# A routed expert kernel: VectorE's order of choosing an expert, reading counts and scaling

## The chip, the cores and the metric

One core of a Trainium2 chip. The number that counts is the device time of one execution in microseconds; of several runs the median is taken. The engines are TensorE (PE in rows, its weight loads PEld), VectorE (DVE), ScalarE (ACT), GpSimd (POOL) and SyncE (SP, which only issues DMAs). Each runs its own instructions in order and waits for others by semaphores.

## What is computed

Attention with keys and values averaged over groups of 8, and behind it a mixture of 8 experts with one expert for each token:

```python
k_p = k.reshape(B, H, Sp, 8, D).mean(axis=3)      # B, H, S, D = 8, 8, 576, 64
v_p = v.reshape(B, H, Sp, 8, D).mean(axis=3)
attn = softmax(scale * q @ k_p^T);  x = attn @ v_p  # as rows: 4608 x 512
logits = x @ w_gate;  expert_idx = argmax(logits)
gate_w = softmax(logits)[expert_idx]
out[mask] = gate_w * (relu(x[mask] @ w1[e]) @ w2[e])   # for each expert e, mask = its tokens
```

## The kernel before, in words

The first stage (`attention`, to about 190 us of the profile) goes through 36 tiles of 128 tokens, nine for each pair of batch elements. Its order is written out by hand (the tile framework is told not to reorder), so the source order is the order on each engine. In the loop from line 542, tile t does this: TensorE transposes the weights P of tile t (`p_transpose`, L283), makes the scores of tile t+2 (L263, into the PSUM tile pS), transposes q of tile t+3 (L253, into pq), does at most one piece of key or value preparation through the PSUM tile pm (`kv_transpose` L180, `v_expand` L207), and multiplies the weights with the values and the folded gate matrix (`weigh`, L299, into pU, of which there is one). VectorE takes the maximum of the scores (L267, tile mx), subtracts it (L270, sd, after which pS is free), then in `scale` takes the reciprocal of the row sums (L311, r), scales the gate logits (L313, lh) and the rows (L315, xe, after which pU is free). ScalarE copies out of PSUM and does the exponentials (L276 from sd).

Tiles come in batches of three for the choice of expert (`route`, after a batch's last tile). VectorE sums the logits, takes the maximum, subtracts it and marks the largest (L374 rg, L375 rm, L376 rd, L378 rk); two more operations, rn (L379) and ro (L346), make the one-hot choice. In the next tile, right behind `weigh`, TensorE counts the tokens of each expert with matmuls of ro (L356, L359, into pm); VectorE adds the running counts (L361 rp, L362 carry), which frees pm, and GpSimd goes on from rp (L387) to the rows' places and the scatter to DRAM (L406). `steps` is a list of small closures; `weave()` runs the next one, and it stands between the larger VectorE operations. `halves` holds pieces of the averaging of keys and values (L172), which VectorE runs behind the subtraction and behind the scaling of rows; GpSimd does other such pieces, right behind its part of the counting. The last three batches are marked `late`, and are ordered in another way that the change leaves alone.

Before the change the first four operations of the choice run at once, and rn and ro are put into `steps`, where the first `weave()` of the next tile runs them, behind that tile's maximum. The counts of the batch are read in the loop of line 601, behind all of `scale`.

The second stage (`experts`) goes through units of up to 512 tokens of one expert, 13 of them in this run. At a unit's start VectorE inverts the gate sums (L1203) and goes on with the hidden layer (L988, each of them behind ScalarE's L967); SyncE loads the rows and gates of later units (`xload`, `gates`, L1238). For the first unit some of this is done by the first stage.

Of the kernel before, what the change touches and what calls it, by code (L numbers as in the profile page):

```python
# [78 lines left out]
def attention(ctx, outer, tc, q, k, v, wg, w1v, w2v, xs, W, cst, carry, tab, banks):  # L79
# [222 lines left out]
    def scale(t):  # L302

        u4 = (pS if t == NG * NT - 2 else pU)[:, :, 0 : 4 * VW].rearrange("p a (h x) -> p a h x", h=4)
        bt, (t0, _) = [(i, b) for i, b in enumerate(batches) if b[0] <= t][-1]
        i = t - t0
        if i == 0:
            xe[bt] = (p3.tile([P, NB, XR], F32, tag="xe", name=f"xe{bt}"), p2.tile([P, NB, NE, H], F32, tag="lh", name=f"lh{bt}"))
        x, lh = xe[bt]
        r = p2.tile([P, 2, 4], F32, tag="r", name=f"r{t}")  # L310
        nc.vector.reciprocal(out=r, in_=u4[:, :, :, D + NE])  # L311
        weave()
        nc.vector.tensor_tensor(out=lh[:, i].rearrange("p e (a h) -> p a h e", a=2), in0=u4[:, :, :, D : D + NE], in1=r.unsqueeze(3).to_broadcast([P, 2, 4, NE]), op=ALU.mult)  # L313
        weave()
        nc.vector.tensor_tensor(out=x[:, i, 0:DM].rearrange("p (a h d) -> p a h d", a=2, h=4), in0=u4[:, :, :, 0:D],  # L315
                                in1=r.unsqueeze(3).to_broadcast([P, 2, 4, D]), op=ALU.mult)
        weave(1, True)


    steps, halves, ready = [], [], []  # L320
    powers, counts = [], []

    def weave(n=1, half=False):
        if half and halves:
            halves.pop(0)()
        for _ in range(min(n, len(steps))):
            steps.pop(0)()

    def route(bt):
        t0, nb = batches[bt]  # L330
        x, lh = (a[:, 0:nb] for a in xe.pop(bt))
        nm = lambda s: f"{s}{bt}"
        bc = lambda a: a.unsqueeze(2).to_broadcast([P, nb, NE])
        t8 = lambda s, dt=F32: p2.tile([P, NB, NE], dt, tag=s, name=nm(s))[:, 0:nb]
        t1 = lambda s: p2.tile([P, NB], F32, tag=s, name=nm(s))[:, 0:nb]
        late = t0 + nb + 3 >= NG * NT
        lg, d, key, oh, pos = t8("rg"), t8("rd"), t8("rk"), t8("ro", BF16), t8("rp")
        m, km, pf = t1("rm"), t1("rn"), t1("rf")
        ex = exs[bt % 2][:, 0:nb]
        ix = p3.tile([P, NB], I32, tag="ix", name=nm("ix"))  # L340

        V = nc.vector
        G = V if late else nc.gpsimd

        def chosen():
            V.tensor_tensor(out=oh, in0=key, in1=bc(km), op=ALU.is_equal)  # L346
            if late:
                power()

        def power():  # L350
            nc.scalar.activation(out=ex[:, :, 0:NE], in_=d, func=AF.Exp)

        def count():
            bank = pm

            nc.tensor.matmul(bank[:, 0 : nb * NE], lhsT=lstrict, rhs=oh.rearrange("p t e -> p (t e)"), start=True, stop=False, skip_group_check=True)  # L356
            for i in range(nb):
                n = nb - i
                nc.tensor.matmul(bank[:, (i + 1) * NE : (nb + 1) * NE], lhsT=ones, rhs=oh[:, i : i + 1, :].to_broadcast([P, n, NE]),  # L359
                                 start=False, stop=i == nb - 1, skip_group_check=True)  # L360
            V.tensor_tensor(out=pos, in0=bank[:, 0 : nb * NE].rearrange("p (t e) -> p t e", t=nb), in1=carry.unsqueeze(1).to_broadcast([P, nb, NE]), op=ALU.add)  # L361
            V.tensor_tensor(out=carry, in0=carry, in1=bank[:, nb * NE : (nb + 1) * NE], op=ALU.add)  # L362
            if bt == AHEAD:
                V.tensor_scalar(out=tab[:, K_AH : K_AH + 1], in0=carry[:, 0:1], scalar1=512.0, scalar2=None, op0=ALU.is_ge)

        def put():
            for i in range(nb):
                nc.gpsimd.tensor_copy(out=ix[:, i : i + 1], in_=pf[:, i : i + 1])  # L368
                scatter(ix[:, i : i + 1], x[:, i, :])
            if bt == AHEAD:  # L370
                ready.append(bt)

        pick = [
            lambda: V.tensor_reduce(out=lg, in_=lh, axis=AX.X, op=ALU.add),  # L374
            lambda: V.tensor_reduce(out=m, in_=lg, axis=AX.X, op=ALU.max),  # L375
            lambda: V.tensor_tensor(out=d, in0=lg, in1=bc(m), op=ALU.subtract),  # L376

            lambda: V.scalar_tensor_tensor(out=key, in0=d, scalar=0.0, in1=cst["order"].unsqueeze(1).to_broadcast([P, nb, NE]), op0=ALU.is_ge, op1=ALU.mult),  # L378
            lambda: V.tensor_reduce(out=km, in_=key, axis=AX.X, op=ALU.max),  # L379
            chosen,  # L380
        ]
        gate = [
            lambda: V.tensor_reduce(out=x[:, :, DM], in_=ex, axis=AX.X, op=ALU.add),
            lambda: G.tensor_copy(out=x[:, :, DM + 1].bitcast(I32), in_=cst["tok"][:, t0 : t0 + nb]),
        ]
        row = [
            lambda: G.tensor_tensor(out=pos, in0=pos, in1=oh, op=ALU.mult),  # L387
            lambda: V.tensor_reduce(out=pf, in_=pos, axis=AX.X, op=ALU.add),
            put,
        ]  # L390
        if late:

            steps.extend([*pick, count, row[0], *gate, *row[1:]])
        else:
            run(pick[:4])
            steps.append(lambda: run(pick[4:]))
            powers.append(power)

            def counted():
                run([count, row[0], gate[1]])  # L400
                steps.extend([gate[0], row[1], put])

            counts.append(counted)

    def scatter(at, rows):
        apart(nc.gpsimd.indirect_dma_start(out=xs, out_offset=bass.IndirectOffsetOnAxis(ap=at, axis=0), in_=rows, in_offset=None))  # L406
# [64 lines left out]
    def run(fs):  # L471
        for f in fs:
            f()
# [68 lines left out]
    for t in range(total):  # L542
# [55 lines left out]
        if held:  # L598
            steps.clear()
        scale(t)  # L600
        for f in counts[:]:
            counts.remove(f)
            f()
            if t in pools:
                run(kv_pool(*pools.pop(t), nc.gpsimd))
        if t == total - 3:
# [104 lines left out]
def experts(ctx, tc, xs, w1v, w2v, out, tab, W, ident, empty, scr, u0, banks):  # L711
# [15 lines left out]
    with tc.tile_critical():  # L727
# [10 lines left out]
        def entry(eng, a, u, lo, hi):  # L738
            r = regs.get((eng, a, u))
            return eng.value_load(tab[u : u + 1, a : a + 1], min_val=lo, max_val=hi) if r is None else r  # L740
# [414 lines left out]
        def dve_unit(u):  # L1155
# [45 lines left out]

            dve.wait_ge(st[u % 2], 64 * (u // 2 + 1))
            dve.reciprocal(out=GT[:, u, :, 0], in_=GT[:, u, :, 0])  # L1203
            n = entry(dve, K_U, u, 1, 8)
            if u > 0:
                hidden_lo(u)
# [18 lines left out]
        def xload(u):  # L1225


            if u == 2:
                sp.wait_ge(se, 16 * (NE - 2))
            if u >= 2:  # L1230
                sp.wait_ge(Q["P_xt"], 4 * (u - 1))

            rows_of = []

            def gates():

                for s in range(4):
                    sp.dma_start(out=GT[:, u, s, :], in_=xs[ds(rows_of[s], P), DM:]).then_inc(st[u % 2], 16)  # L1238

            def block(s, apart, rows=True):  # L1240
                r = rows_of[s]
                to, sem = XE[u % 2][:, s, :], sx[u % 2][s]
                if rows and apart:
                    for j in range(4):
                        o = slice(32 * j, 32 * j + 32)
                        sp.dma_start(out=to[o].rearrange("p (g d) -> p g d", g=4),
                                     in_=xs[ds(r, P), j * P : (j + 1) * P].rearrange("(g t) d -> t g d", g=4)).then_inc(sem, 16)
                elif rows:
                    sp.dma_start(out=to, in_=xs[ds(r, P), 0:DM]).then_inc(sem, 16)
                    sp.sem_inc(sem, 48)  # L1250
                else:
                    sp.sem_inc(sem, 64)

            rows_of.extend(entry(sp, K_ROW + s, u, 0, NE * CAP - P) for s in range(4))
            n = entry(sp, K_U, u, 1, 8)

            def blocks(apart):
                for s in range(2):
                    block(s, apart)
                with sp.If(n > 4):  # L1260
                    block(2, apart)
                    with sp.If(n > 6):
                        block(3, apart)
                    with sp.Else():
                        block(3, apart, False)
                with sp.Else():
                    for s in range(2, 4):
                        block(s, apart, False)

            if u < 2:  # L1270
                blocks(False)
                return gates()
            with sp.If(entry(sp, K_U, u - 1, 1, 8) > 2):
                blocks(True)
            with sp.Else():
                blocks(False)
            gates()
# [247 lines left out]
```

## Time and profile before

| | us |
|---|---|
| median of 3 runs | 635.15 |
| lowest and highest | 633.09, 635.31 |
| the profiled execution's own time | 631.38 |
| its span | 629.6 |
| TensorE busy in the span | 602.3 |

The span is what the profiler sees from the first to the last instruction; the execution's time is 1.8 us longer. A row of the timeline gives start, duration, engine, line, operation, what it writes and reads; in square brackets stands how long the engine stood idle before it, and who ended that. A matmul's duration includes the emptying of the array, and consecutive ones overlap, so the distance of starts says more than the durations.

### The profile page before, as it was taken

The page shows a single profiled execution, that of the slowest core. Times are in us where ns is not written, and L with a number is a line of the kernel's source. Part 1 is how long each engine was busy: PE and PEld are TensorE (multiplying, and loading weights), DVE is VectorE, ACT ScalarE, POOL GpSimd, SP SyncE. Part 2 cuts the span into 40 slices and gives each one's busy share as a digit, 9 for nine tenths or more (in the row PEclk, how much of TensorE's full clock was granted, in tenths as well). Part 3 has the DMA queues.
Part 4 walks back from the last instruction along what each step waited for, and adds up shares of the span by engine and source line. Part 5 has one row for each costly group of instructions (what it writes and reads, how often), then busy time and mean ns, then how long its engine had stood idle before and what let it go on. Part 6 is the DMA issues. An engine that isn't in the chain of part 4 may idle for free.

```text
span 629.6 us, 13468 instructions
## 1 busy us (share of the span) xinstructions
PE 602.3 (96%) x4412; PEld 513.0 (81%) x4412; DVE 354.4 (56%) x731; ACT 240.2 (38%) x453; POOL 240.7 (38%) x289
## 2 busy tenths in 40 slices
PE   6989999999997999999999999999998999999995
PEld 6778978888876888889898889888897888888994
DVE  7698887889762124467777433854156664133220
ACT  2577666886512014065354311523034641011110
POOL 7457656744421121468445311251107660101101
PEclk9999999999999999999999999999999899999999
DMA  9999996992324930619667551075105453100001
GB/s 326 363 267 258 300 311 209 254 265 70 125 111 135 300 107 2 216 41 297 221 173 267 153 170 36 3 210 167 40 33 164 132 147 71 55 0 36 36 4 53
DMA packets 93937, 96.47 MB, mean 153 GB/s; under 512 B 43102, under 2 KB 74846, under 8 KB 93792
## 3 DMA queue, kind: packets, MB, share of 16 engines
q1 hardware_dynamic: 85808, 74.27, 41.0%
q0 software_dynamic: 7440, 20.50, 8.8%
q8 instruction: 60, 0.98, 0.6%
q14 instruction: 85, 0.70, 0.4%
q10 hardware_dynamic: 544, 0.02, 0.0%
HBM read 72.68 MB, written 26.00 MB: 157 GB/s over the span
## 4 chain that ended last, share of the span: by engine, by line
PE 76%; DVE 6%; issue 5%; DMA 3%; POOL 3%; ACT 3%; SPq 2%; DVEq 0%; ACTq 0%; POOLq 0%
PE pU L881 33%; PE pP L859 20%; PE pq L859 10%; PE pU L299 4%; DMA XE<-in_v_dram 2%; PE pP L283 2%; PE pP L462 2%; POOL dispatched L406 2%; PE pS L263 2%; PE pq L253 1%; SPq L228 1%; ACT W L1057 1%; PE pm L207 1%; DVE mx L267 1%; PE pq L462 1%
## 5 line engine op out<-in xcount | busy, mean ns | idle before, releaser
L881 PE MATMUL pU<-W,H 128*128 128x512 f32 x912 | 216.2, 397 | 0.0
L881 PEld LDWEIGHTS pU<-W,H 128*128 128x128 f32 x912 | 171.3, 188 | 41.0
L859 PE MATMUL pP<-X,W 128*128 128x512 f32 (+3 forms) x748 | 144.0, 347 | 3.7 <-DVEq L1398 1.5
L859 PEld LDWEIGHTS pP<-X,W 128*128 128x128 f32 x748 | 123.6, 189 | 20.4 <-DVEq L1398 2.0
L1349 POOL DMA_INDIRECT out_dram<-Y,GT x51 | 53.0, 1039 | 193.3 <-DVE Y L1170 167.4
L1065 POOL TENSOR_TENSOR W<-ST,W 128x1024 fp32r<-128x1024 f32 x30 | 77.4, 2591 | 89.9 <-ACT W L1057 89.4
L967 ACT ACTIVATE H<-pP 128x512 fp32r<-128x512 f32 (+1 forms) x67 | 35.9, 536 | 196.7 <-PE pP L859 158.1
L1170 DVE TENSOR_SCALAR Y<-pU,GT 128x512 f32<-128x512 f32 x36 | 26.9, 749 | 110.5 <-PE pU L881 109.0
L988 DVE SCALAR_TENSOR_TENSOR H<-pP,H 128x512 fp32r<-128x512 f32 (+2 forms) x73 | 42.1, 579 | 71.5 <-ACT H L967 69.0
L859 PE MATMUL pq<-X,W 128*128 128x512 f32 (+3 forms) x364 | 73.7, 351 | 1.1 <-DVE H L988 0.6
L859 PEld LDWEIGHTS pq<-X,W 128*128 128x128 f32 x364 | 60.8, 191 | 10.1 <-DVE H L988 1.1
L1057 ACT CAST W<-ST 128x1024 fp32r<-128x1024 f32 x56 | 57.1, 1054 | 2.9 <-DMA ST<-in_moe_w_dram 2.9
L299 PE MATMUL pU<-V,pt 110*128 110x146 f32 (+3 forms) x468 | 56.7, 283 | 1.4 <-ACT pt L284 0.8
L299 PEld LDWEIGHTS pU<-V,pt 110*128 110x128 f32 (+3 forms) x468 | 51.4, 179 | 3.1 <-ACT pt L284 1.8
L1065 DVE TENSOR_TENSOR W<-ST,W 128x1024 fp32r<-128x1024 f32 x26 | 46.8, 1801 | 3.5 <-ACT W L1057 2.5
L967 ACT ACTIVATE H<-pq 128x512 fp32r<-128x512 f32 (+1 forms) x33 | 17.8, 541 | 79.5 <-PE pq L859 55.1
L406 POOL DMA_INDIRECT dispatched<-xe,ix x36 | 38.0, 1054 | 15.6 <-POOL ix L368 7.0
L988 DVE SCALAR_TENSOR_TENSOR H<-pq,H 128x512 fp32r<-128x512 f32 (+2 forms) x35 | 20.8, 595 | 28.2 <-ACT H L967 20.3
L284 ACT COPY pt<-pP 110x384 f32<-110x384 f32 x72 | 30.8, 479 | 6.1 <-PE pP L283 4.9
L276 ACT ACTIVATE P<-sd 128x576 f32<-128x576 f32 x36 | 24.8, 689 | 19.3 <-DVE sd L270 16.2
L172 POOL TENSOR_TENSOR raw<-raw 128x768 f32<-128x768 f32 (+1 forms) x18 | 27.0, 1498 | 12.1 <-DMA raw<-in_v_dram 11.4
L267 DVE TENSOR_REDUCE mx<-pS 128x8 f32<-128x576 f32 x36 | 27.1, 752 | 6.8 <-PE pS L263 4.4
(186 smaller groups left out, 621.8 us busy)
## 6 DMA issues: line engine op xcount, KB each, us to landing
ST<-in_moe_w_dram SPq DMA_DIRECT2D x56, 512.0 KB, 4.6
raw<-in_k_dram SPq DMA_DIRECT2D x12, 768.0 KB
raw<-in_v_dram SPq DMA_DIRECT2D x11, 768.0 KB
XE<-dispatched SPq DMA_DIRECT2D x104, 64.0 KB, 2.0
qa<-in_q_dram SPq DMA_DIRECT2D x24, 256.0 KB
w<-in_moe_w_dram SPq DMA_DIRECT2D x8, 512.0 KB
XE<-dispatched SPq DMA_DIRECT2D x15, 256.0 KB, 3.8
qa<-in_q_dram SPq DMA_DIRECT2D x2, 1024.0 KB
```

Source lines behind the costliest of these rows:

```text
L172: return lambda: eng.tensor_tensor(out=out, in0=raw[:, :, 0:n], in1=raw[:, :, n : 2 * n], op=ALU.add)
L267: nc.vector.tensor_reduce(out=mx, in_=s4, axis=AX.X, op=ALU.max)
L284: take(out=pt[t][a][0:R], in_=pPs[a][0:R, 0 : 3 * P])
L299: nc.tensor.matmul(pu[p0 : p0 + n, a, h * VW : (h + m) * VW], lhsT=pt[t][a][0:r, c % 3 * P + p0 : c % 3 * P + p0 + n], rhs=Vs[g % 2][0:r, ...
L406: apart(nc.gpsimd.indirect_dma_start(out=xs, out_offset=bass.IndirectOffsetOnAxis(ap=at, axis=0), in_=rows, in_offset=None))
L859: r = pe.matmul(out=pH[g % 3][:, :m], lhsT=w1s(w, f, k), rhs=x, start=i == 0, stop=i == len(passes) - 1)
L881: r = pe.matmul(out=pY[:, s % 2, :], lhsT=h, rhs=w[:, k * 512 : (k + 1) * 512], start=start and i == 0, stop=stop and i == len(ps) - 1, sk ...
L967: act.activation(out=HH[:, f, o], in_=src[:, o], func=AF.Relu).then_inc(Q["A_h"], 1)
L988: return dve.scalar_tensor_tensor(out=dst[:, f, to], in0=src[:, at], scalar=0.0, in1=f32(HH[:, f, at]), op0=ALU.max, op1=ALU.subtract)
L1057: act.copy(out=(W1H if i < 4 else W2H)[:, o], in_=ST[:, i, :]).then_inc(Q["A_s1" if i < 4 else "A_s2"], 1)
L1065: eng.tensor_tensor(out=(W1L if i < 4 else W2L)[:, o], in0=ST[:, i, :], in1=f32((W1H if i < 4 else W2H)[:, o]), op=ALU.subtract).then_inc( ...
L1349: pool.indirect_dma_start(out=out, out_offset=bass.IndirectOffsetOnAxis(ap=GT[:, u, s, 1:2].bitcast(I32), axis=0), in_=Y[:, s, :], in_offs ...
```

## The change

The whole choice is made at once behind the batch's last tile. The counts are read behind the reciprocal of the next tile, ahead of scaling logits and rows; what follows the counts (the `tails`) goes into `steps` where it went before. In the second stage a drain is put behind the inversion of the gate sums, and SyncE waits for a unit's first hidden piece before it loads the gates of the unit after the next.

```diff
@@ scale(t)
         nc.vector.reciprocal(out=r, in_=u4[:, :, :, D + NE])
+        for f in counts:
+            f()
         weave()
         nc.vector.tensor_tensor(out=lh[:, i]..., op=ALU.mult)
@@ route(bt), batches that are not late
-            run(pick[:4])
-            steps.append(lambda: run(pick[4:]))
+            run(pick)
             powers.append(power)
-
-            def counted():
-                run([count, row[0], gate[1]])
-                steps.extend([gate[0], row[1], put])
-
-            counts.append(counted)
+            counts.append(lambda: run([count, row[0], gate[1]]))
+            tails.append([gate[0], row[1], put])
@@ the loop over tiles
         scale(t)
-        for f in counts[:]:
-            counts.remove(f)
-            f()
+        if counts:
+            counts.clear()
+            steps.extend(tails.pop())
             if t in pools:
                 run(kv_pool(*pools.pop(t), nc.gpsimd))
@@ dve_unit(u)
             dve.reciprocal(out=GT[:, u, :, 0], in_=GT[:, u, :, 0])
+            dve.drain()
@@ gates()
+                if u >= 2:
+                    sp.wait_ge(Q["V_h"], 8 * (u - 2) + 1)
                 for s in range(4):
                     sp.dma_start(out=GT[:, u, s, :], ...)
```

## Rows read from the trace of the kernel before

**Rows 1.** The page: busy us, share of the span and instructions of each engine.
```profile
PE 602.3 (96%) x4412; PEld 513.0 (81%) x4412; DVE 354.4 (56%) x731; ACT 240.2 (38%) x453; POOL 240.7 (38%) x289
```

**Rows 2.** Busy time by stretch: the stretch in us, its length, busy us and instructions of each engine, granted clock, share of DMA engines, GB/s.
```profile
38.00:60.00 22.00, 19.37 (x302) 16.56 (x301) 20.39 (x54) 15.44 (x35) 14.17 (x18) 1.00 1.00 261
118.00:146.00 28.00, 26.58 (x412) 23.22 (x413) 24.50 (x64) 23.10 (x49) 14.70 (x21) 1.00 0.73 212
190.00:630.00 440.00, 426.92 (x2068) 359.45 (x2068) 200.63 (x314) 127.00 (x210) 137.21 (x98) 0.99 0.39 117
```

**Rows 3.** What TensorE waited for from 20 to 190 us: who waited, for whom, us in total, times, longest.
```profile
PE pm L356 <- DVE ro L346: 2.2, 2, 1.2
PE pm L207 <- DVE carry L362: 1.4, 4, 0.5
PE pm L180 <- POOL rp L387: 1.3, 3, 0.5
```

**Rows 4.** Timeline of the batch that is counted at 57 us, TensorE's rows: start, duration, engine, line, operation.
```profile
52.74 0.66 PE L253 MATMUL pq<-ident,qa 128*128 128x128 f32 x4
53.23 1.61 PE L299 MATMUL pU<-V,pt 110*128 110x146 f32 x12
54.84 0.17 PE L356 MATMUL pm<-ro,lstrict 128*128 128x24 bf16 x1
55.71 0.73 PE L263 MATMUL pS<-kT,qT 64*64 64x72 f32 x32
56.38 0.66 PE L253 MATMUL pq<-ident,qa 128*128 128x128 f32 x4
57.50 0.90 PE L207 MATMUL pm<-wrhs,vT 128*110 128x144 f32 x6 [0.47 <-DVE carry L362]
58.24 1.66 PE L299 MATMUL pU<-V,pt 110*128 110x146 f32 x12
```

**Rows 5.** The same stretch, VectorE's and GpSimd's rows.
```profile
53.63 0.18 DVE L378 SCALAR_TENSOR_TENSOR rk<-rd,order 128x24 f32<-128x24 f32 x1
53.73 0.75 DVE L267 TENSOR_REDUCE mx<-pS 128x8 f32<-128x576 f32 x1
54.40 0.17 DVE L379 TENSOR_REDUCE rn<-rk 128x3 f32<-128x24 f32 x1
54.60 0.18 DVE L346 TENSOR_TENSOR ro<-rk,rn 128x24 bf16<-128x24 f32 x1
54.70 0.75 DVE L270 TENSOR_TENSOR sd<-pS,mx 128x576 f32<-128x576 f32 x1
55.83 0.20 DVE L311 RECIPROCAL r<-pU 128x8 f32<-128x8 f32 x1
56.80 0.35 DVE L172 TENSOR_TENSOR kvp<-raw 128x192 f32<-128x192 f32 x1
57.07 0.18 DVE L361 TENSOR_TENSOR rp<-pm,carry 128x24 f32<-128x24 f32 x1
57.28 0.16 DVE L362 TENSOR_TENSOR carry<-carry,pm 128x8 f32<-128x8 f32 x1
57.65 2.89 POOL L172 TENSOR_TENSOR raw<-raw 128x768 f32<-128x768 f32 x2
59.93 0.21 DVE L311 RECIPROCAL r<-pU 128x8 f32<-128x8 f32 x1 [0.94 <-PE pU L299]
```

**Rows 6.** Timeline of the batch that is counted at 94 us.
```profile
91.26 0.76 DVE L267 TENSOR_REDUCE mx<-pS 128x8 f32<-128x576 f32 x1 [1.39 <-PE pU L299]
92.37 0.17 PE L356 MATMUL pm<-ro,lstrict 128*128 128x24 bf16 x1 [1.16 <-DVE ro L346]
93.25 0.73 PE L263 MATMUL pS<-kT,qT 64*64 64x72 f32 x32
```

**Rows 7.** Timeline around the count at 119 us: ScalarE's copies and TensorE behind them.
```profile
118.21 1.03 ACT L423 CAST W<-w 128x1024 fp32r<-128x1024 f32 x1
119.15 0.85 ACT L284 COPY pt<-pP 110x384 f32<-110x384 f32 x2
120.06 1.48 PE L299 MATMUL pU<-V,pt 110*64 110x146 f32 x24
```

**Rows 8.** Timeline around the count at 131 us.
```profile
128.29 1.72 PE L299 MATMUL pU<-V,pt 110*128 110x146 f32 x12 [0.81 <-ACT pt L284]
130.06 0.17 PE L356 MATMUL pm<-ro,lstrict 128*128 128x24 bf16 x1
132.41 0.85 ACT L284 COPY pt<-pP 110x384 f32<-110x384 f32 x2
```

**Rows 9.** VectorE's additions for the averages of keys while GpSimd does such additions too (the first two), and of the same size without them (the third; for the second the one of [rows 5]).
```profile
38.84 1.21 DVE L172 TENSOR_TENSOR raw<-raw 128x384 f32<-128x384 f32 x1
48.60 0.78 DVE L172 TENSOR_TENSOR kvp<-raw 128x192 f32<-128x192 f32 x1
55.37 0.55 DVE L172 TENSOR_TENSOR raw<-raw 128x384 f32<-128x384 f32 x1
```

**Rows 10.** The second stage by line: the gate inversion, the drains that are there already (count, shortest, median and longest in ns), and what VectorE waited for ahead of the hidden layer (us, times).
```profile
L1203 DVE RECIPROCAL GT<-GT x13: 157/170/179, 199.4 to 589.9; 128x4 f32<-128x4 f32 x13
L1165 DVEq DRAIN  x3: 697/765/1894, 285.5 to 502.0; - x3
  ACT H L967: 89.3, 56
```

More of the change, by code (lines that the diff above doesn't have):

```diff
@@ L320, in attention @@
     steps, halves, ready = [], [], []
-    powers, counts = [], []
+    powers, counts, tails = [], [], []
     def weave(n=1, half=False):
```

## The prediction

> **What bounds the kernel now.** I read the page first: TensorE is busy 96% of the span, the others 56% or less [rows 1]. So a VectorE reorder is worth something only where TensorE stands still for VectorE. The windows come next. Behind 190 us, in the second stage, TensorE is busy 426.92 of 440 us and VectorE less than half [rows 2]; nothing of the first stage's edits runs there. In the first stage TensorE is nearly full, but VectorE is too: 20.39 of 22 us from 38 to 60, and 24.50 of 28 us from 118 to 146, where ScalarE has 23.10 [rows 2]. The waits of TensorE between 20 and 190 us then name what this change touches: the count's matmul for the one-hot choice ro, 2.2 us in two waits, and the next piece of key or value preparation for the counts to be read out of pm, 1.4 and 1.3 us in seven waits [rows 3]. That is seven of ten batches that aren't late, and the rest wait for nothing listed there.
>
> The reader should see in the timeline that the list is too low. In the batch at 57 us, q's transposes start at 56.38 and L207 at 57.50, a distance of 1.12; undisturbed, from 52.74 to 53.23, it is 0.49 [rows 4]. The delay is 0.63, the listed wait 0.47: each is 0.16 short, the modelled end of a matmul. Seven such delays make 2.7 + 7 x 0.16 = 3.8 us. The two waits for ro make 2.2 + 2 x 0.16 = 2.5 us, and there are smaller ones below the list: at 131 us the twelve matmuls of the product take 1.77 from the first start to the count's [rows 8], against 1.45 undisturbed (their 1.61 of [rows 4] less those 0.16), so 0.32; I put four such at this bound, 1.3 us in all. **The ceiling of the gain is 3.8 + 2.5 + 1.3 = 7.6 us.**
>
> **Reading the counts early.** Nothing is added or removed: per batch, two VectorE operations of 0.18 and 0.16 move from behind the scaling of rows and the kvp addition to right behind the reciprocal [rows 5]. In the batch at 57 us carry ended at 57.44. With the reciprocal starting at 55.83, and 0.23 later for the reason below, the two end near 56.6, before the transposes of q have gone by at 56.38 + 0.49 = 56.87. So the wait for pm goes completely, 0.63 there. The count's matmuls, at 54.84, are done long before, so the two reads bring no new wait on TensorE in such a tile; if VectorE were ahead of TensorE, the first would wait for the count's matmuls of 0.17 [rows 4], which stand right behind the product. What is queued behind them on VectorE is the scaling of logits and rows, about 0.35 later; the scaling of rows frees pU for the next product. It ended about where kvp started, at 56.80, and would now end near 56.80 + 0.23 + 0.35 = 57.4; that product could start at 58.24 - 0.63 = 57.6, so it fits, by 0.2. On GpSimd the mask, the token copy and then the key additions come in the same order, some 0.7 earlier; the scatters keep their place in `steps`, and no DMA is moved past another on the queue of SyncE or GpSimd.
>
> **Making the choice at once.** rn and ro move ahead of the maximum. On VectorE the order rk, mx, rn, ro, sd takes from rk at 53.63 to sd at 54.70, 1.07 [rows 5]. In the new order dependent operations stand side by side: 0.20 to rn, 0.20 to ro, 0.10 until mx, and then mx's 0.75 and 0.04 until sd, 1.29 or so. So ro is ready 0.6 earlier, but **sd comes 0.23 later** wherever VectorE goes from rk straight on. sd frees pS for the next scores. At 57 us sd ended at 55.45 and the scores started at 55.71; with sd ending at 55.68 they start no earlier than now. So the 0.15 that the count's matmul gains is given back at once. Where VectorE instead stood waiting ahead of the maximum, as at 91.26 for 1.39, sd comes 0.2 earlier and the scores of 93.25 follow [rows 6]: of that wait of 1.32, about 0.4 is kept.
>
> **The sum, over ten batches.** The seven waits on pm give 3.8. From this goes the first batch, at 45 us: there VectorE is nearly without a gap [rows 2], so what TensorE gains it waits for at the next sd: -0.65. At 119 us, ScalarE has a weight copy of 1.03 between, and the product at 120.06 starts only 0.9 behind the start of the pt copies at 119.15 [rows 7]; these hang on sd, which is later, so about 0.4 of 0.55 is lost. Added is 0.4 at 92 us. The batch at 131 us and the one behind it had no wait on pm, and there the pt copies at 132.41 [rows 8] let the next product start; they come 0.2 later: -0.4 for both. The last batch gives nothing. 3.8 - 0.65 - 0.4 + 0.4 - 0.4 = 2.75, **2.8 us**.
>
> **The second stage.** A drain stands behind each of 13 inversions of 0.17 [rows 10]. The trace has no drain behind an inversion. From below: nothing, or a gain of none, since it removes no work. From above: the longest drain there is, 1.9 us, 13 times, 25 us of VectorE. I take the length of the operation drained, about 0.2, so 2 us in all, because the drains that are there last about as long as what stands ahead of them. What hides it is the wait for ScalarE ahead of the hidden layer, 89.3 us in 56 times [rows 10], over 1 us each; without that cover it would cost these 2 us. Nothing goes into the sum. SyncE's wait for the first hidden piece of the unit two before holds up the gate loads and behind them weight loads, which themselves wait for later work of the same unit; the gates are needed a whole unit later, so I take nothing; its price, if late, is bounded by one hidden piece, 1.6 us (89.3 / 56), and by none below.
>
> The profiled execution took 631.38; the sum gives 628.6. It lies 3.8 below the median of the runs shown, 635.15, so against that I say **632.3 us**. About 0.5%, 3.2 us, is what a measurement of this kernel can tell from no change, so the forecast lies just inside "the same".
>
> **Rivals.** *All waits go.* If sd and the pt copies have more room than I read, the whole 7.6 us is saved: 627.5. For it: TensorE is the busiest engine, and VectorE stands idle 0.94 ahead of the reciprocal one tile later [rows 5]. Against it: the scores at 55.71 start 0.26 behind sd's end. *Given back.* VectorE paces the first stage, its work is the same, and 0.23 more of gaps per batch; each gain is lost at the next pS, and 0.3 us remain: 634.9. For it the busy shares of 38 to 60 and 118 to 146 us [rows 2]; against it that same 0.94. *Slower by collision.* GpSimd's key additions now start some 0.7 earlier and meet VectorE's kvp addition, which now comes behind the scaling. Such an addition took 0.78 beside GpSimd's and 0.35 [rows 5] without, a larger one 1.21 against 0.55 [rows 9]. Five batches at 0.43, one with a larger addition at 0.7 to 0.8, and ten times 0.23 make 5.2 us on VectorE. It decides when VectorE's delay in the tile, 0.1 + 0.43, and TensorE's gain, 0.63, together pass the 0.94: they do, by 0.2, which the next maximum's room should take. If it doesn't, and the waits on pm return as waits on sd, half of the 5.2 to all of it is lost: 637.8 to 640.4; I take two thirds, 638.6, as the batches are alike. The Trainium skill, "Advanced Engine Details and Errata", section "VectorE Performance Modes", notes that the second VectorE port into SBUF is shared with GpSimd and that their instructions block each other, which is the mechanism of this rival; it limits it to the two-port modes, while the rows show it for f32 additions of two tensors. By that limit the collision would cost nothing here, and the forecast would stand. *The change does nothing* is not likely, as both moves are plain in program order; it falls in with "given back".
>
> **The numbers.** Forecast 0.52, all waits go 0.15, given back 0.24, collision 0.09. The forecast's own range is 630.5 to 634.0: a gain of 1.2 if the delay of 0.23 is lost in all seven batches with a wait on pm besides (2.8 - 1.6), of 4.6 if the three losses of the sum don't come and twice as much is kept at 92 us (2.75 + 1.45 + 0.4). The range that takes in "all waits go" and "given back" is 627.4 to 635.7. Faster by over 0.5%: 0.15 and 0.23 of the forecast's 0.52, 0.38. Same: 0.29 + 0.24 = 0.53. Slower: 0.09.
>
> **What would show it.** Right: TensorE's waits for carry, rp and ro vanish from its list; L361 starts right behind the reciprocal; sd follows the maximum without rn and ro between; the first stage ends about 2.8 us earlier and the second is as long as before. Step by step wrong: waits of the scores on sd or of the product on pt, in place of the old ones and as long; kvp additions of 0.7 us in most batches; a drain in front of a late hidden piece. The forecast is wrong if the first stage gains over 4.6 or nothing.

## The result, and the profile after

The changed kernel took **642.47 us** (median of 7 runs, 640.16 to 648.09) against 635.15 for the kernel before beside it: ratio 1.0126, 95% interval 1.0101 to 1.0151. By the medians it is slower by 7.3 us where 2.8 us less were forecast, and outside the range. The ratios here and below are worked out from the single runs, without the few that were disturbed, and differ a little from the quotients of the medians.

In the profiled execution the span is 646.4 us against 629.6, and 14.0 of these 16.8 us lie in the first stage: the trace by line gives the start of the second stage's first product (the range behind the durations in ns); before, the same line (L881 there) began at 200.0 us.

```profile
L878 PE MATMUL pU<-W,H x912: 390/397/632, 214.0 to 639.8; 128*128 128x512 f32 x183
```

The profiled execution is the slowest of the seven, 648.09 us, and that of the kernel before, 631.38, is faster than any of its runs beside, so the difference of the two traces is more than that of the medians. Part of the 14.0 us is the clock: in two stretches in the middle of the first stage TensorE was granted 0.50, its lower level, 1.2 GHz. The columns are those of [rows 2].

```profile
81.30:88.10 6.80, 6.80 (x78) 6.00 (x73) 6.45 (x19) 3.93 (x9) 1.72 (x3) 0.50 0.44 147
98.40:105.20 6.80, 6.80 (x61) 6.22 (x60) 6.42 (x16) 2.63 (x7) 3.32 (x5) 0.50 0.90 226
```

They are not the cause: the same program lost 1.45, 0.93 and 1.12% in later runs whose traces have no such stretch between 50 and 200 us (e5, e11, e16).

TensorE's waits from 20 to 203 us answer to [rows 3]. Those for carry and for GpSimd's rp are gone, as forecast; in their place stand the scores waiting for the subtraction sd, which frees pS.

```profile
PE pS L263 <- DVE sd L270: 6.9, 10, 2.2
PE pU L299 <- ACT pt L284: 2.5, 5, 0.8
PE pq L253 <- ACT qr L248: 1.4, 3, 0.5
PE pS L263 <- DVE rf L390: 1.4, 3, 0.5
PE pm L358 <- DVE ro L348: 0.6, 1, 0.6
```

VectorE by line, 20 to 190 us (busy us, mean ns of one, idle before them and what ended it), first in the kernel before, then in the changed one:

```profile
L267 DVE TENSOR_REDUCE mx<-pS 128x8 f32<-128x576 f32 x35 | 26.3, 752 | 6.8 <-PE pS L263 4.4 <-PE pU L299 1.4 <-PE pm L207 0.5
L172 DVE TENSOR_TENSOR kvp<-raw 128x192 f32<-128x192 f32 x10 | 3.9, 393 | 0.0
```

```profile
L267 DVE TENSOR_REDUCE mx<-pS 128x8 f32<-128x576 f32 x35 | 26.2, 750 | 14.4 <-PE pm L180 4.3 <-PE pm L207 3.9 <-PE pP L283 3.4
L172 DVE TENSOR_TENSOR kvp<-raw 128x192 f32<-128x192 f32 x10 | 9.7, 969 | 0.0
```

Two things are new there. The ten additions for the keys take 9.7 us; before, they took 3.9. And VectorE stands idle 14.4 us ahead of the maximum, before 6.8. Before, 4.4 of it were ended by the scores' own matmuls (L263); now most of it is ended by instructions of TensorE (L180, L207, L283) that come after the scores in its order. The maximum reads nothing of theirs; it reads pS, whose matmuls had begun long before. The timeline of the batch counted at 57 us ([rows 4, 5]) and of the tile behind it shows both:

```profile
57.07 0.20 DVE L311 RECIPROCAL r<-pU 128x8 f32<-128x8 f32 x1
57.19 0.13 DVE L363 TENSOR_TENSOR rp<-pm,carry 128x24 f32<-128x24 f32 x1
57.36 0.16 DVE L364 TENSOR_TENSOR carry<-carry,pm 128x8 f32<-128x8 f32 x1
57.73 2.88 POOL L172 TENSOR_TENSOR raw<-raw 128x768 f32<-128x768 f32 x2
58.17 1.59 DVE L172 TENSOR_TENSOR kvp<-raw 128x192 f32<-128x192 f32 x1
59.68 0.75 DVE L267 TENSOR_REDUCE mx<-pS 128x8 f32<-128x576 f32 x1
60.46 0.76 DVE L270 TENSOR_TENSOR sd<-pS,mx 128x576 f32<-128x576 f32 x1
61.36 0.73 PE L263 MATMUL pS<-kT,qT 64*64 64x72 f32 x32 [0.41 <-DVE rf L390]
61.83 1.04 POOL L403 DMA_INDIRECT dispatched<-xe,ix  x1 [0.28 <-POOL ix L370]
63.35 0.97 POOL L403 DMA_INDIRECT dispatched<-xe,ix  x1 [0.28 <-POOL ix L370]
63.99 0.76 DVE L267 TENSOR_REDUCE mx<-pS 128x8 f32<-128x576 f32 x1 [1.72 <-PE pm L207]
```

The counts are read right behind the reciprocal, as planned. GpSimd's first key addition starts at 57.73, VectorE's at 58.17 within it, and it takes 1.59 us in place of 0.35. The scores then wait for VectorE (0.41), and the scatter of the batch's first rows starts 0.47 behind their first matmul. The scores are 0.73 us long, but the maximum starts only at 63.99, after 1.72 us of idleness. In an undisturbed tile it starts 0.29 us behind the start of the last score matmul. Below, a maximum is called *late* when VectorE waited over 0.35 us for it and it began over 0.6 behind that start; between 45 and 130 us this trace has five (1.72, 3.38, 2.60, 2.21, 1.71), the kernel before three (0.54, 1.39, 0.51). Two causes were to be told apart: VectorE's longer additions, alone (C) or together with the later sd (S: each is absorbed, both are not), and the late maxima, as a trouble of their own (L) or brought on where GpSimd's scatters lie against the scores (P, for phase).

### The profile page after: what moved, and what is told of

Same layout as the page of the kernel before. It is cut to its first block, busy times and chain, and to the rows that moved or that the text cites. A ratio compares the mean times of both kernels' runs of the same rounds, so it can differ in the third digit from the quotient of the medians.

```text
span 646.4 us, 13497 instructions
## 1 busy us (share of the span) xinstructions
PE 610.4 (94%) x4412; PEld 520.6 (81%) x4412; DVE 362.8 (56%) x731; ACT 239.5 (37%) x453; POOL 240.9 (37%) x289
## 4 chain that ended last, share of the span: by engine, by line
PE 72%; DVE 14%; issue 4%; DMA 4%; ACT 3%; SPq 1%; POOL 1%; DVEq 0%; ACTq 0%; POOLq 0%
PE pU L878 33%; PE pP L856 19%; PE pq L856 10%; DVE mx L267 2%; PE pU L299 2%; DVE raw L172 2%; DVE sd L270 2%; DMA XE<-in_v_dram 2%; PE pP L459 2%; DVE xe L317 1%; DMA XE<-dispatched 1%; PE pP L283 1%; PE pS L263 1%; ACT W L1054 1%; PE pq L253 1%
## 5 line engine op out<-in xcount | busy, mean ns | idle before, releaser
L299 PE MATMUL pU<-V,pt 110*128 110x146 f32 (+3 forms) x468 | 59.8, 291 | 3.2 <-ACT pt L284 2.5
L299 PEld LDWEIGHTS pU<-V,pt 110*128 110x128 f32 (+3 forms) x468 | 53.9, 186 | 5.7 <-ACT pt L284 4.6
L263 PE MATMUL pS<-kT,qT 64*64 64x72 f32 x1152 | 28.3, 235 | 9.6 <-DVE sd L270 6.9
L263 PEld LDWEIGHTS pS<-kT,qT 64*64 64x64 f32 x1152 | 22.8, 138 | 17.5 <-issue 12.8
L267 DVE TENSOR_REDUCE mx<-pS 128x8 f32<-128x576 f32 x36 | 27.0, 750 | 14.4 <-PE pm L180 4.3
```

What stands on the lines that cost most here:

```text
L263: nc.tensor.matmul(pS[p0 : p0 + 64, hp, j * SK : (j + 1) * SK], lhsT=qT[t][r, j * P + p0 : j * P + p0 + 64], rhs=kTs[g % 2][r, b, j, hp * ...
L267: nc.vector.tensor_reduce(out=mx, in_=s4, axis=AX.X, op=ALU.max)
L299: nc.tensor.matmul(pu[p0 : p0 + n, a, h * VW : (h + m) * VW], lhsT=pt[t][a][0:r, c % 3 * P + p0 : c % 3 * P + p0 + n], rhs=Vs[g % 2][0:r, ...
```

## The experiments

They ran on five chips, A to E, always beside the kernel before. The table puts them together: median in us, ratio to the kernel before on the same chip with its interval; then from the profiled execution late maxima with their idle time, the ten kvp additions from 20 to 190 us, and the start of the second stage (each in us).

| run | chip | this; before | ratio | late | kvp | second stage from |
|---|---|---|---|---|---|---|
| e1 changed, VectorE's addition first | A | 631.96; 630.11 | 1.0019 (0.9999 to 1.0040) | 1: 0.6 | 3.6 | 198.7 |
| e2 counts only | A | 629.88 | 0.9995 (0.9977 to 1.0014) | 0 | 9.7 | 197.0 |
| e3 choice only | A | 631.51 | 1.0024 (1.0005 to 1.0044) | 0 | 3.9 | 200.8 |
| e4 second stage only | A | 629.77 | 0.9992 (0.9967 to 1.0016) | 0 | 3.9 | 197.2 |
| e5 changed | B | 643.80; 635.20 | 1.0145 (1.0107 to 1.0184) | 5: 10.1 | 9.7 | 210.6 |
| e6 changed, first stage only | B | 644.88 | 1.0157 (1.0115 to 1.0200) | 5: 7.9 | 9.7 | 207.8 |
| e7 counts, addition first | B | 631.28 | 0.9938 (0.9919 to 0.9957) | 4: 2.5 | 3.6 | 198.4 |
| e8 counts only | C | 635.19; 634.09 | 1.0043 (1.0009 to 1.0077) | 5: 6.4 | 9.7 | 202.0 |
| e9 choice only | C | 634.85 | 1.0020 (0.9999 to 1.0041) | 2: 1.8 | 3.9 | 202.9 |
| e10 changed, addition first | C | 635.20 | 1.0010 (0.9990 to 1.0030) | 4: 4.1 | 3.6 | 202.5 |
| e11 changed | C | 638.57 | 1.0093 (1.0058 to 1.0128) | 5: 5.6 | 9.7 | 205.0 |
| e12 changed | D | 631.74; 630.34 | 1.0020 (1.0007 to 1.0033) | 0 | 9.7 | 199.9 |
| e13 changed, scatter later | D | 631.68 | 1.0025 (1.0011 to 1.0038) | 0 | 9.7 | 199.6 |
| e14 counts, addition first | D | 630.04 | 1.0002 (0.9978 to 1.0025) | 0 | 3.5 | 196.8 |
| e15 the same, scatter later | D | 629.82 | 0.9985 (0.9967 to 1.0003) | 0 | 3.5 | 197.2 |
| e16 changed | E | 642.20; 634.48 | 1.0112 (1.0064 to 1.0160) | 6: 7.5 | 9.7 | 207.9 |
| e17 changed, scatter later | E | 633.88 | 0.9982 (0.9960 to 1.0004) | 0 | 9.7 | 200.5 |
| e18 counts, addition first, scatter later | E | 635.91 | 1.0017 (0.9988 to 1.0047) | 6: 6.7 | 3.6 | 202.4 |

**The parts, one by one (A).** e1 is the changed kernel with VectorE's own key addition ahead of the counts, so that it is over when GpSimd's begins:

```diff
         nc.vector.reciprocal(out=r, in_=u4[:, :, :, D + NE])
+        if counts and halves:
+            halves.pop(0)()
         for f in counts:
             f()
```

> The changed kernel, but in the tile that reads the counts VectorE runs its addition for the averages (kvp, once raw) right behind the reciprocal, ahead of reading the counts; all else as changed. Collision (VectorE's addition stands behind the whole of GpSimd's first addition: 1.59 instead of 0.35 us in five tiles, 2.19 instead of 0.95 in one): the additions are back to 0.35 and 0.95, and the time is below the kernel before, 630 to 634 us. Late subtraction (the choice ahead of the maximum delays sd by 0.2 us in ten tiles): 641 to 643, as changed, since sd stays late. Second stage (drain and SyncE's wait): 641 to 643.

e2 has only the early counts; the choice is split around the maximum as before (`run(pick[:4])`, the rest in `steps`). e3 has only the choice (`run(pick)`), the counts where they were. e4 has only the two lines of the second stage (`dve.drain()` and the wait of SyncE).

> The kernel before with the early reading of the counts alone; choice of expert and second stage as before. Collision: nearly all of the loss, 640 to 643 us. Late subtraction: 632 to 635, as the waits for pm go and sd isn't late. Second stage: 632 to 635.

> The kernel before with the whole choice of expert ahead of the next maximum alone; counts and second stage as before. Collision: 634 to 636, no change. Late subtraction: 639 to 642. Second stage: 634 to 636.

> The kernel before with the drain behind the gate inversion and SyncE's wait ahead of the gate loads alone. Collision and late subtraction: 634.5 to 636.5, at most 1 us more than before. Second stage: 639 to 643.

The second stage's edits cost nothing (e4). The collision is whole in e2, 9.7 us of additions, and e2 loses nothing: six more us of VectorE's work alone are absorbed. The choice costs 1.4 us; TensorE's list of e3 from 20 to 190 us shows for it the scores waiting for sd and the product for the scaled rows:

```profile
PE pU L299 <- DVE xe L315: 1.4, 2, 0.8
PE pS L263 <- DVE sd L270: 1.3, 2, 0.7
```

So on A no part explained a loss of 7 us, and the changed kernel itself had not run there, so that e1 alone settles nothing. There the kernel before took 630, not 635 us, and no trace but e1's has a late maximum.

**The whole, and without the second stage (B).** e5 is the changed kernel again, e6 the same without the two lines of the second stage, e7 the kernel before with early counts and VectorE's addition ahead of them (the lines of e1), the choice behind the maximum.

> The changed kernel, unaltered, beside its parts' chip. Sum of parts (the single edits measured -0.2, +1.4 and -0.3 us beside before): 1 us more than before, ratio 1.000 to 1.004. Together (the collision of additions is harmless alone and costs only when the subtraction is late too, both in one tile): 5 to 9 us more than before, ratio 1.008 to 1.014, with waits of the scores on sd of 5 us and more in TensorE's list. Late signals (in the first profile of the changed kernel VectorE's maximum waited five times 1.7 to 3.4 us for scores that TensorE had begun 2.1 to 3.8 us before): ratio above 1.008 only if such waits are there in this trace, and 1.000 to 1.005 if they aren't.

> The changed kernel without the second stage's edits (no drain, no wait of SyncE). Sum of parts: 1 us more than before. Together and late signals: as the changed kernel beside it, within 1 us, since the second stage's edits are not part of either. Second stage: 3 us or more below the changed kernel.

> The kernel before with the counts read early and VectorE's addition for the averages ahead of them, behind the reciprocal; choice and second stage as before: neither a collision nor a late subtraction. Collision harmless alone: as with the counts alone, ratio 0.997 to 1.001. Collision costs something even without the late subtraction: 2 to 4 us below before, ratio 0.993 to 0.997.

The loss came back with e5 and e6, with five late maxima each, so the sum of the parts, about 1 us, is refuted. "Together" and "late signals" both fit: e5 has the late maxima, and waits of the scores for sd of 5.8 us from 20 to 190 us. e7, without collision or moved choice, was 3.9 us below the kernel before and had late maxima of at most 0.82.

**The design on one chip (C).** The four kernels e8 to e11 are those of e2, e3, e1 and e5.

> The kernel before with only the counts read ahead of scaling logits and rows; the choice stays behind the maximum. A second run of this kernel, on the same chip as the next three. Theory S (the two parts spend the same slack: the collision with GpSimd's key addition, 1.24 us a batch, and the subtraction 0.2 us later are each absorbed and together are not): no loss alone, ratio 0.99 to 1.002, with 1.59 us additions and TensorE's waits for sd under 3 us between 20 and 203 us. Theory L (VectorE learns late of TensorE's scores, and whatever moves VectorE's work into the stretch of GpSimd's scatters pays for it): a loss of 3 to 6 us wherever the kernel before takes about 635 us, none where it takes about 630.

> The kernel before with only the whole choice of expert ahead of the next tile's maximum. Theory S: a small loss, 0 to 2 us, as the subtraction comes 0.2 us later and no addition collides. Theory L: as the counts are read where they were, the same stalls as in the kernel before, so 0 to 2 us as well where it takes 630 us, and 3 us and more where it takes 635 us, if the moved choice itself is what meets the scatters.

> The changed kernel with VectorE's key addition ahead of the counts, so that it is over when GpSimd's begins; the choice stays ahead of the maximum. Theory S: without the collision the changed kernel's loss goes, to within 2 us of the kernel before. Theory L: the stalls stay, and with them 4 us or more of the loss where the kernel before takes 635 us.

> The changed kernel as it is, beside the three above on one chip. Theory S: 7 to 9 us over the kernel before on any chip, since the collision and the moved choice are the program's. Theory L: 7 to 9 us where the kernel before takes 635 us, but no more than 2 us, the loss of the choice alone, where it takes 630 us and no late maximum is in the trace.

Theory S put the whole loss into the pair and expected none from the counts alone; they cost 0.43% here (0.09 to 0.77), nothing on A. Theory L fits that, but e10 refutes its claim that 4 us of the loss stay. e11 lost 5.9 us by its ratio, less than the 7 to 9 that both expected. What goes with the loss is the collision, though only on a chip with late maxima.

**Where the late ones lie.** This changed the question: what is at work when a maximum comes late? In 12 traces, ten from B, C and E and the two of the result, 50 late maxima lie between 45 and 130 us. In 45 of them GpSimd was in a scatter's record 0.29 us behind the start of the last score matmul, when the maximum was due; in the other 5 one had ended less than 0.5 us earlier. (36 more were due within a scatter: 33 began later for VectorE's own work, 3 were in time.) Of the maxima due with no scatter in the last 0.5 us not one is late: 29 began within 0.6, the others when VectorE was done with something else. On A and D, 18 due within a scatter began within 0.6, and one was late by 0.64. There the same overlap is nearly harmless.

**Shifting the scatter alone (D, then E).** e13 and e17 are the changed kernel, collision and all, with four idle casts on GpSimd ahead of each batch's first index; they start the scatters, and what GpSimd does behind them, 0.5 us later and touch nothing of VectorE or TensorE. e15 and e18 have them in the kernel of e7, e12 and e16 are the changed kernel, e14 is that of e7. (The expectations put the shift at 0.75 us; the four casts ran closer together.)

```diff
+            for i in range(4):
+                nc.gpsimd.tensor_copy(out=spare[:, i : i + 1], in_=pf[:, 0:1])
             for i in range(nb):
                 nc.gpsimd.tensor_copy(out=ix[:, i : i + 1], in_=pf[:, i : i + 1])
                 scatter(ix[:, i : i + 1], x[:, i, :])
```

> The changed kernel as it is, as the control of the next run on the same chip. Both theories: 5 to 10 us over the kernel before where its maxima come late (1 to 2 us in each of five batches); about 1.5 us over it if this chip shows no late maximum.

> The changed kernel with four idle casts of 0.19 us on GpSimd ahead of each batch's first index, so that the three scatters start 0.75 us later; the collision with the key addition stays, 1.59 us in five batches. Theory P (phase: TensorE's finished scores are seen late when they end inside a scatter, and the collision puts them there): the first late maximum of each batch goes (idle 0.3 us in place of 1 and more), at most a smaller one at the next tile stays, and the time falls by 2 to 5 us against the changed kernel. Theory C (VectorE's longer additions are the cost themselves): the time stays within 1 us of the changed kernel's, or is longer by the casts.

> The kernel before with the counts read ahead of logits and rows and VectorE's key addition ahead of the counts; the choice stays behind the maximum. It was 3.9 us below the kernel before on one chip. Both theories: again 2 to 4 us below it (TensorE's waits for the counts are gone, no collision, the subtraction not delayed); within 1 us of it if the forecast saving of 2.75 us was never there and the first run was the chip's.

> The same kernel as e14 with the four idle casts ahead of each batch's first index. Theory P: where e14's late maxima (0.5 to 0.8 us, three or four of them) sit in the scatter's stretch, shifting it removes some and may make others, so within 1.5 us of e14 either way, with the idle of the maxima going along with the time. Theory C: same as e14 or slower by up to 1 us for the casts.

D showed no late maximum, and there the changed kernel is 1.4 us slower, as much as its choice alone on A, with the collision whole (9.7 us). This is already against theory C, alone or as S, since both parts are in the program; the shift had nothing to mend. e14 and e15 did not bring the 2 to 4 us expected of them, and lie within 0.5 us of the kernel before. E did show late maxima:

> The changed kernel as it is, control of the next run. If the chip shows late maxima: 5 to 10 us over the kernel before, with the maximum 1.3 us or more behind the last score matmul in the first tile after a batch's counts. If not: 1.5 us over it.

> The changed kernel with four idle casts on GpSimd ahead of each batch's first index; on another chip the scatter then began 0.28 to 0.44 us behind the last score matmul in place of 0.04 to 0.3 us ahead of it. Theory P (a scatter under way when the scores end makes the maximum late): in the tiles where the scatter now begins behind the scores, the maximum comes 0.3 us after them, and the time falls by 2 us or more against e16 where e16 has late maxima; equal where it has none. Theory C (the cost is VectorE's longer additions): equal to e16 within 1 us in any case, and the maxima as late as in e16.

> Counts read early behind VectorE's key addition, choice where it was, and the four idle casts. Below the kernel before by 3 us or more where that one takes about 635 us, equal to it within 1.5 us where it takes about 630 us, if the early counts save what was forecast only where the maxima come late; 2.75 us below it on any chip if the forecast term holds everywhere.

e17 took 633.88 us where the unshifted program took 642.20: **the loss is gone**, the ratio to the kernel before is 0.9982, with the additions at 9.7 us in both. Here is the same tile in e16,

```profile
61.57 0.17 DVE L390 TENSOR_REDUCE rf<-rp 128x3 f32<-128x24 f32 x1
61.80 0.73 PE L263 MATMUL pS<-kT,qT 64*64 64x72 f32 x32 [0.41 <-DVE rf L390]
62.26 1.04 POOL L403 DMA_INDIRECT dispatched<-xe,ix  x1 [0.28 <-POOL ix L370]
63.67 0.76 DVE L267 TENSOR_REDUCE mx<-pS 128x8 f32<-128x576 f32 x1 [0.96 <-PE pq L253]
63.73 0.59 ACT L255 COPY qT<-pq 128x512 f32<-128x512 f32 x1 [0.55 <-PE pq L253]
```

in e17, with the casts,

```profile
60.59 0.17 DVE L393 TENSOR_REDUCE rf<-rp 128x3 f32<-128x24 f32 x1
60.82 0.73 PE L263 MATMUL pS<-kT,qT 64*64 64x72 f32 x32 [0.41 <-DVE rf L393]
60.82 0.55 POOL L371 CAST spare<-rf 128x1 int32<-128x1 f32 x4
61.64 0.75 DVE L267 TENSOR_REDUCE mx<-pS 128x8 f32<-128x576 f32 x1
61.76 1.04 POOL L406 DMA_INDIRECT dispatched<-xe,ix  x1 [0.28 <-POOL ix L373]
62.17 0.59 ACT L255 COPY qT<-pq 128x512 f32<-128x512 f32 x1
```

and in e12, the program of e16 on chip D:

```profile
61.10 0.73 PE L263 MATMUL pS<-kT,qT 64*64 64x72 f32 x32 [0.41 <-DVE rf L390]
61.56 1.03 POOL L403 DMA_INDIRECT dispatched<-xe,ix  x1 [0.28 <-POOL ix L370]
61.93 0.75 DVE L267 TENSOR_REDUCE mx<-pS 128x8 f32<-128x576 f32 x1
62.45 0.59 ACT L255 COPY qT<-pq 128x512 f32<-128x512 f32 x1
```

From the scores' first matmul to the maximum: 1.87 us, 0.82, 0.83. The scatter starts 0.46, 0.94 and 0.46 behind that first matmul. In e16 ScalarE's copy of qT is held too, so it is not VectorE that is busy with something unseen: two engines that wait for TensorE's signals go on at nearly the same moment, 63.67 and 63.73.

The traces also hold the moment at which each semaphore update arrived, which none of these rows shows, and there the lateness can be seen itself. In e16 the last score matmul is recorded as ending at 62.53 and the last transpose of q at 63.11; their updates arrived at 63.64 and 63.70. In e12 the scores ended at 61.83 and the update arrived at 61.88. Behind the scores TensorE's records keep the same pace in both: the last matmuls of the next three groups start 0.54, 1.21 and 2.66 us behind the last score matmul in e16, 0.53, 1.20 and 2.65 in e12. So TensorE was not held; its signals were. In the same 12 traces, between 45 and 130 us, 827 of TensorE's updates were due while no scatter was under way or had ended in the last 1 us, and 826 of them arrived within 0.1 us; of the 406 due within a scatter 254 came later or have no record, and so did 89 of the 207 due within 1 us behind one. Of VectorE's updates due within a scatter it is 93 of 448, of ScalarE's 89 of 334. On A and D the three shares within a scatter are 25 of 269, 7 of 377 and 11 of 242.

Why the changed kernel sits at just this distance shows in the same rows: with VectorE late, rf follows sd without a gap; the scores start 0.23 behind rf's start (61.57 to 61.80) and the index and the scatter follow rf by a fixed 0.69. Both hang on VectorE, so their distance hardly changes: in the five batches of e16 from 60 to 120 us the first scatter starts 0.46 or 0.47 us behind the scores' first matmul four times and 0.30 once. Before, the scores did not wait for VectorE and the scatter started later, past the signal, by 1.14 to 1.37 us in the same five batches; only in the second tile behind a batch did a maximum come late.

```profile
60.48 0.73 PE L263 MATMUL pS<-kT,qT 64*64 64x72 f32 x32
61.62 1.03 POOL L406 DMA_INDIRECT dispatched<-xe,ix  x1 [0.28 <-POOL ix L368]
```

The shift is no cure in general. In e18 it took the second tile's scores into a scatter, six were late (0.55 to 1.53), and it lost to its expectation of 3 us saved. A row of that trace fits the rule badly: the scores begin at 64.76, a scatter ended at 65.23 and the next started 0.2 behind the scores' recorded end, and the maximum came 0.5 behind the end of the second.

```profile
64.26 0.97 POOL L409 DMA_INDIRECT dispatched<-xe,ix  x1 [0.28 <-POOL ix L375]
64.76 0.73 PE L263 MATMUL pS<-kT,qT 64*64 64x72 f32 x32
65.70 0.98 POOL L409 DMA_INDIRECT dispatched<-xe,ix  x1 [0.28 <-issue]
67.16 0.76 DVE L267 TENSOR_REDUCE mx<-pS 128x8 f32<-128x576 f32 x1 [0.97 <-PE pm L207]
```

So the recorded stretch of a scatter is not exactly the stretch that delays. The Trainium skill, "Perfetto Trace Analysis", section "DMA Instruction — SWDGE (GPSIMD)", says that such a record ends when GpSimd has generated the descriptors and not when the data has moved. No run here tells which of the two holds the signals.

## Why the prediction was wrong, step by step

**Reading the counts early.** The waits on pm went, as forecast. Their worth, 2.75 us net, did not hold. On A and D no late maxima stand in the way (e1's apart). There e4, with the first stage of the kernel before, has these waits, 0.7 and 1.3 us (TensorE, 20 to 190 us):

```profile
PE pm L180 <- POOL rp L387: 1.3, 3, 0.5
PE pm L356 <- DVE ro L346: 1.1, 1, 1.1
PE pm L207 <- DVE carry L362: 0.7, 2, 0.4
```

and in e14 those for rp and carry are gone, without collision and without the moved choice. Its ratio to the kernel before is 1.0002 (0.9978 to 1.0025), where 2.75 us are 0.0044. The last score matmul of its tile at 120 us is 1.35 us earlier than e4's (119.06 against 120.41, two chips), that of the last tile 0.96, its second stage only 0.4 (196.8 against 197.2): by these two traces about half of the term was there and most of that was lost again. Part of the rest may be the clock, as e14 has a stretch at half clock from 195.2 us and e4 none there. TensorE's list names what it waits for instead:

```profile
PE pU L299 <- ACT pt L284: 1.3, 3, 0.8
PE pm L360 <- DVE ro L350: 0.9, 1, 0.9
PE pS L263 <- DVE sd L270: 0.9, 1, 0.9
```

e4 has 0.8 for pt and 0.3 for sd. So this part went much as the rival "given back" has it, by the ratio. e7's -3.9 us on B is larger than the forecast, but without a trace of the kernel before on B the share of it that is fewer late maxima can't be told; that stays open.

**Making the choice at once.** Put at no loss beyond 0.23 per batch, with +0.4 and -0.4 among the terms. Measured: 1.5 us by the ratio on A (e3, 0.3 to 2.8) and 1.3 us on C (e9, -0.1 to 2.6, so not clear of noise), in e3 as waits on sd and the rows. The size is off by about one us, in the direction that the rival gave.

**The collision.** The rival had the place, the sign and the engine, and was given 0.09. Its price was too low: 0.43 per addition, measured 1.59 - 0.35 = 1.24 in five batches. The addition of 0.78 in [rows 9], at 48.60, had met a short addition of GpSimd's (48.57 to 49.16 in the same trace) and ended 0.22 behind it. In the changed kernel the one at 58.17 meets GpSimd's first addition of 57.73 to 59.54, and again ends 0.22 behind it: what it costs is what is left of GpSimd's instruction. The Trainium skill, "Advanced Engine Details and Errata", names only the two-port modes for this blocking in the section "VectorE Performance Modes", and the prediction took that for a limit; its section "GPSIMD Details" names VectorE instructions with two SBUF inputs as well. These runs agree with the latter, for an f32 addition of two SBUF operands, 0.35 us alone and 1.59 beside GpSimd. Yet the way it was to cost time was wrong too: on A and D this added work, 6 us, costs nothing that can be measured (e2; e12 loses no more than the choice alone does), and in e17 it costs nothing where e16 loses 7.7. It costs by its phase.

**What failed.** The step that failed is the sentence that the scatters "keep their place in `steps`", by which they got no term in the sum. Their place in the order stayed, their time against the scores did not: 0.46 us behind the first score matmul in place of 1.14 and more, and five or six maxima late by 5.6 to 11.6 us in all where the changed kernel lost. And the row that told it was read as something else: the maximum at 91.26 that waited 1.39 [rows 6] was counted as room that VectorE has, worth +0.4. In the trace of before its scores begin at 88.45 while a scatter runs from 88.30 to 89.26 and another from 89.74 to 90.73: it is a late maximum, one of three, and the kernel before is paying there already.

```profile
88.30 0.96 POOL L406 DMA_INDIRECT dispatched<-xe,ix  x1 [0.28 <-POOL ix L368]
88.45 0.73 PE L263 MATMUL pS<-kT,qT 64*64 64x72 f32 x32
89.74 0.99 POOL L406 DMA_INDIRECT dispatched<-xe,ix  x1 [0.28 <-issue]
```

The update of these scores, whose last matmul is recorded as ending at 89.18, arrived at 91.23. That may be part of why the kernel before took 634 to 635 us on B, C and E and 630 on A and D; its first stage ended at 200.0 in the result's trace and at 197.2 in e4, which has the same first stage.

**The second stage** was forecast at nothing, and is nothing (e4; e6 against e5). The drains themselves were mis-sized: 0.19 to 0.87 us each in the result's trace, median 0.64, where 0.2 was taken. They still cost nothing that can be measured.

The sum as measured on E: 7.7 us of loss by the medians with the scatter in phase, -0.6 with it shifted (by the ratio -1.1, interval -2.5 to +0.3). On D it is 1.4, the choice. Six late maxima of 1.0 to 1.7 us, 7.5 in all, come to as much as the difference of 7.4 in the start of the second stage between e16 and e17 (207.9 and 200.5).

## What to carry to other kernels

Ask of every wait whether the instruction named had been done long before, and what else ran at that moment. A releaser later than the operand's producer, as L207 for a maximum that reads pS, can mark a signal that came late rather than slack. When a change makes one engine release both a consumer chain and a DMA issue, it can fix their distance for every iteration, so a rare collision can become one per batch: compare the phases, not the order alone. And an addition that shares an engine pair's memory must be priced by what is left of the other's instruction that it starts in.

## What the runs showed of the hardware

Scatters issued by GpSimd went with late signals of TensorE to VectorE and ScalarE, and moving the scatters took the late maxima away (e17). The maxima waited 0.4 to 3.4 us for them on three of the five chips and in the result's runs, and hardly on the other two (18 on time, one late by 0.64). The same program, the kernel before, took 4 to 5 us longer on the former; how much of that is late signals is not shown. What differs between the chips, and whether the generation of the descriptors or the transfer of the rows holds the signals, was not tried. One sign of a difference is in the traces: the 12 of the former hold 217 to 230 records of updates for the 231 of TensorE's instructions that send one, the eight from A and D at least 231. Each execution timed here has a span and a clock from the profiler, so no run shows whether signals come late without its recording. Version e7 is the only one that came out clearly below the kernel before (0.9938 on B), but the same on D (1.0002); no kernel here beats it on every chip. The first half-clock stretch of the result's profile began at 81.3 us, behind the maximum that was 3.38 us late (it began at 79.24); in the other traces of the changed kernel there was none between 50 and 200 us.
